# Moving the set-up of the first exponents to VectorE, and a new order, in an mLSTM step followed by a two-layer MLP on one core

## The chip, the cores and the metric

The kernel runs on one core of a Trainium2 chip. The time is device microseconds (us) of that core, the median of three runs. The core's engines work side by side and meet through semaphores: TensorE (PE) multiplies matrices and writes PSUM, VectorE (DVE) and ScalarE (ACT) do elementwise work, GpSimd (POOL) some masks and set-up, and SyncE (SP) issues the DMAs. A release in the profile is an engine, or a DMA, that another one had waited for.

## The reference

First an mLSTM recurrence over 768 steps for 4 batches and 8 heads of 40 numbers, with a running maximum `m` that keeps the exponents in range; its 3072 x 320 output goes through an MLP with 2048 hidden columns.

```python
for t in range(S):
    m_new = np.maximum(f_gate[:, :, t] + m, i_gate[:, :, t])
    f_stab = np.exp(f_gate[:, :, t] + m - m_new)
    i_stab = np.exp(i_gate[:, :, t] - m_new)
    m = m_new
    C = f_stab * C + i_stab * np.einsum('bhd,bhe->bhde', vt, kt)
    n = f_stab * n + i_stab * kt
    y[:, :, t] = sigmoid(o_gate) * (C @ qt) / np.maximum(np.abs(n @ qt), 1.0)
h = x @ w_in                      # x: y as 3072 x 320
g = h * erf(softplus(h))
out = g @ w_out
```

The weights come as 64-bit words. The kernel decodes them to 32 bits on VectorE and ScalarE.

## The kernel before

The 768 steps are cut into 12 chunks (steps) `c` of 64. A step's work for batches 0 and 1, and for 2 and 3, are its halves `r` = 0 and 1. In `attention(c)` the recurrence becomes matrix products: `scores` multiplies q and k into `S`; VectorE multiplies `S` by `dm`, the exponentials of gate differences (L681); `before` adds what the state of earlier steps gives, and the next state's part (L635, L640); `heads` multiplies by v (L649). Then VectorE divides (`den`, L710 to L718), applies the output gate (L724), and copies the last 64 columns of each row once more (L725), so that three 128-wide transposes (`turned`, L510) can bring the result into the layout of the MLP. ScalarE and VectorE split each transposed result into a high and a low part, `xh` and `xl` (L519, L523), since the products run in a format with fewer bits: two or three products replace one.

`mlp(g)` takes 48 groups: four per step, each with a quarter `q` of the hidden columns. A group is two up-projections of 16 matmuls into `h` (L858), two copies `hb` (L866), softplus and erf on ScalarE (L870, L874; each table change costs an ACT_TABLE_LOAD), a multiplication on VectorE (L878), a split into `gh` and `gl`, and the down products into the banks of `pob`, one per 128 tokens: L919 and L920 (`gh`) and L917 (`gl`). The first six groups (`PLAIN`) aren't split and use L915. After a step's last quarter ScalarE copies the bank into `o` (L925), and two DMAs bring it out. Each weight block `raw` is decoded by L740, L746, L751 and L753 and split by L763 and L767 (`w_in`; L801 and L805 for its last 64 rows) or L827 and L831 (`w_out`).

Steps 0 and 1 make their exponents by a matmul of `lt` and `xd` (L562), whose operands `gate_block(0)` builds on VectorE from the gates `gt`, with the selectors `sel`, `one` and `heads_of`. Later steps send theirs through DRAM (`gd`) and read them back as `dm` and `eT`.

The order of all engines' instructions is computed when the kernel is built. `Plan` lists operations with an engine, a cost, what they read and write and a due time, and runs them through a list scheduler: at each moment every free engine takes the ready operation that is due first. `SHIFT`, a table with a number per part and engine, is added to the due times. For TensorE, `fetch` counts instructions: each `BLOCK` of them takes at least `FETCH` us before the next can begin. Where TensorE would be idle for more than `GAP`, `fillers` says how many matmuls on `ident` are put in (`stay`, L983); before the first down product one of them is 128x512. Each engine runs its instructions strictly in the order that results.

At the start GpSimd makes `one` (L355, L357), `ident`, `m0` and `keep` (L347 to L349), zeroes `state` (L384) and then computes `sel` from the constants `cst` (L362 to L370). ScalarE finishes `one` with it (L375), VectorE makes `heads_of` (L379).

Of the kernel before, what the change touches and what calls it, by code (L numbers as in the profile page):

```python
# [10 lines left out]
F32 = mybir.dt.float32  # L11
# [23 lines left out]
class Plan:  # L35
# [5 lines left out]
    GAP, FILL, WIDE_FILL = 0.9, 0.6, 0.85  # L41
    BLOCK, FETCH, SPREAD, SAME = 634, 5.0, 8.0, 1.0
# [84 lines left out]
    def run(self, switch, stay=None):  # L127
# [9 lines left out]
        self.block = 0, -10.0  # L137
# [22 lines left out]
        while count < n:  # L160
# [19 lines left out]
            for e in ('PE', 'DVE', 'ACT', 'POOL', 'SP'):  # L180
# [46 lines left out]
                if e == 'PE':  # L227
                    opened = opened or bool(o.name) and o.name[:2] == 'dn'
                    gap = now - idle
                    if gap > self.GAP and idle > 0:  # L230
                        at, begun = self.block
                        at += 10 * self.fillers(gap, opened)
                        self.block = (at % self.BLOCK, now) if at >= self.BLOCK else (at, begun)
                    if mode is not None and o.kind != mode:
                        cost += 0.2
                    mode = o.kind
                    end, self.block = self.fetch(now, cost, o.mm)
                    cost = end - now
                    idle = end
# [33 lines left out]
WIN = [50, 50, 50, 50, 50, 50]  # L273
WOUT = [50, 50, 50, 50]
LAG = 9.772298661887838
STEPS = [0.39055807994090763, 48.51524298161213, 47.54329309094079, 80.07669209656675, 112.61009110219268, 145.14349010781865, 177.67688911344462, 210.21028811907055, 242.7436871246965, 275.27708613032246, 307.8104851359484, 340.34388414157434]
FIRST, FIRST_X = ((0, 1), (2, 3), (4, 5), (6, 7)), (2, 3)
EACH, LAST = ((0, 1), (2, 3)), ((0, 1), (2,), (3,))
PLAIN, JOIN, GH_ACT = 6, 3, 16


def nominal(g):
    return FIRST_DUE[g] if g < 8 else FIRST_DUE[7] + EVERY * (g - 7)


@with_exitstack
def tile_mlstm_moe(
# [41 lines left out]
    keep = cp.tile([128, W], F32, name="keep")
    one = cp.tile([128, 2, L], F32, name="one")  # L330
    sel = cp.tile([128, 4 + B], F32, name="sel")
    heads_of = cp.tile([128, H], F32, name="heads_of")
    state = [cp.tile([128, 2, NPR, V1], F32, name=f"state{r}") for r in range(2)]
    wh = cp.tile([128, 3, DFF], F32R, name="wh")
    wl = cp.tile([128, 2, DFF], F32R, name="wl")
    woh = cp.tile([128, NFF, DM], F32R, name="woh")

    accs = []
    pob = ps.tile([128, 2, 512], F32, name="pob")

    @dma(6, w=[('cst', 0)], due=-900.0)
    def _():
        nc.sync.dma_start(cst, consts)

    @op('POOL', 0.2, w=[('m0', 0)])
    def _():
        nc.gpsimd.memset(m0, -1e30)  # L347
        nc.gpsimd.memset(keep, 1.0)
        nc.gpsimd.memset(keep[:, L:L + 1], 0.0)  # L349

    @op('POOL', 2.2, w=[('one', 0)], due=-80.0)
    def _():
        for b in reversed(range(B)):
            rows = 32 * (b + 1)
            nc.gpsimd.memset(one[0:rows], 0.0)  # L355
            for i, (test, fill) in enumerate(((ALU.not_equal, 1.0), (ALU.is_ge, -1e30))):
                nc.gpsimd.affine_select(out=one[0:rows, i], in_=one[0:rows, i], pattern=[[1, L]],  # L357
                                        compare_op=test, fill=fill, base=16 * b + 16, channel_multiplier=-1)

    @op('POOL', 1.3, r=[('cst', 0)], w=[('is', 0)], due=-70.0)  # L360
    def _():
        nc.gpsimd.tensor_tensor(sel[:, 1:2], cst[:, 9:10], cst[:, 8:9], op=ALU.subtract)  # L362
        nc.gpsimd.tensor_tensor(sel[:, 0:1], cst[:, 10:11], cst[:, 8:9], op=ALU.add)
        nc.gpsimd.tensor_tensor(sel[:, 2:3], sel[:, 0:1], sel[:, 1:2], op=ALU.add)
        nc.gpsimd.tensor_scalar(out=sel[:, 3:4], in0=sel[:, 2:3], scalar1=-1.0, scalar2=1.0, op0=ALU.mult, op1=ALU.add)
        of = sel[:, 4:4 + B]
# [49 lines left out]
    def gate_block(c):  # L416
# [4 lines left out]
        @dma(128, w=[(('gt', c), 0)], tile_=('gt', ('gt', c)))  # L421
        def _():
            nc.sync.dma_start(new('gt', [128, 2, W], ('gt', c)), gates[:, :, rows])
# [626 lines left out]
```

## Time and profile before

| what | us |
|---|---|
| median of three runs (480.41 to 481.48) | 481.37 |
| the profiled execution, its own time | 479.99 |
| its span | 478.3 |
| TensorE busy, share of the span | 456.3, 95% |
| VectorE busy | 322.0, 67% |
| ScalarE busy | 313.6, 66% |
| GpSimd busy | 48.2, 10% |
| granted TensorE clock, mean | 0.993 |

A share over the whole span hides that stages differ. A later table gives the busy time by stage; there, an engine whose busy time fills the stage sets the pace in it. In a group's row stand the line, the engine, the operation, what is written `<-` what is read, the count, then the busy time, the mean ns of one, and the idle time before it with what ended it. Matmuls overlap one another, so their mean ns is more than what one adds. A float32 matmul is recorded twice, so a filler has two records.

### The profile page before, as it was taken

The numbers are of one execution on the slowest core, as the hardware profiler recorded it, in microseconds if no ns is written. First come the engines' busy times: TensorE is split into PE (matmuls) and PEld (weight loads), VectorE is DVE, ScalarE is ACT, GpSimd is POOL, SyncE is SP. The second block draws the span as 40 slices with busy tenths as digits, with TensorE's granted clock in tenths as the row PEclk, the third lists the DMA queues.
The fourth block names the chain that finished last, engine by engine and source line by source line (L and its number), as shares of the span: only waits on it lengthen the run. The fifth ranks groups of instructions, "written<-read, shape, count | busy, mean of one in ns | idle before, by whom it ended". The sixth has DMA issues, their size and how long they took to land.

```text
span 478.3 us, 14687 instructions
## 1 busy us (share of the span) xinstructions
PE 456.3 (95%) x6482; PEld 421.5 (88%) x6482; DVE 322.0 (67%) x574; ACT 313.6 (66%) x433; POOL 48.2 (10%) x71
## 2 busy tenths in 40 slices
PE   6788999899999999999999999999999999999996
PEld 2457878678999999999899999999999999999985
DVE  4889999999988378367639557769069551554280
ACT  3636799948598399648179288396287272894760
POOL 4000002101203003002101101104003100000000
PEclk9979999999999999999999999999999999999999
DMA  8997835332362433033324313604040300000011
GB/s 282 313 307 224 270 123 170 105 116 78 115 169 66 134 128 129 18 116 107 93 108 128 104 29 108 171 14 143 7 127 21 116 16 1 2 14 15 1 27 29
DMA packets 42476, 50.77 MB, mean 106 GB/s; under 512 B 22700, under 2 KB 27308, under 8 KB 42412
## 3 DMA queue, kind: packets, MB, share of 16 engines
q1 hardware_dynamic: 42412, 49.83, 34.6%
q8 instruction: 51, 0.84, 0.7%
q14 instruction: 13, 0.11, 0.1%
HBM read 45.68 MB, written 4.13 MB: 104 GB/s over the span
## 4 chain that ended last, share of the span: by engine, by line
PE 82%; DVE 8%; ACT 7%; issue 2%; POOL 1%; POOLq 0%; ACTq 0%; DVEq 0%
PE h L858 35%; PE pob L919 10%; PE pob L917 10%; PE pob L920 9%; PE pa L649 3%; PE pob L983 3%; PE pa L635 2%; PE pa L626 2%; PE pob L915 2%; PE pa L915 2%; ACT L985 2%; DVE raw L751 1%; PE pa L510 1%; PE pa L640 1%; ACT n L870 1%
## 5 line engine op out<-in xcount | busy, mean ns | idle before, releaser
L858 PE MATMUL h<-xh,wh 128*128 128x256 f32 x576 | 159.6, 288 | 0.0
L858 PE MATMUL h<-xl,wh 128*128 128x256 f32 x576 | 156.7, 283 | 0.0
L858 PEld LDWEIGHTS h<-xh,wh 128*128 128x128 f32 x576 | 110.0, 191 | 1.9 <-ACT hb L866 0.6
L858 PEld LDWEIGHTS h<-xl,wh 128*128 128x128 f32 x576 | 110.2, 191 | 0.7 <-DVE vg L614 0.2
L866 ACT ACTIVATE hb<-h 128x512 f32<-128x512 f32 x96 | 56.4, 593 | 81.9 <-PE h L858 81.8
L858 PE MATMUL h<-xh,wl 128*128 128x256 f32 x384 | 108.6, 283 | 0.1
L919 PE MATMUL pob<-woh,gh 128*128 128x320 f32 x328 | 99.4, 315 | 1.6 <-ACT o L925 1.6
L920 PE MATMUL pob<-wo,gh 128*128 128x320 f32 x328 | 97.5, 309 | 0.0
L878 DVE TENSOR_TENSOR n<-n,hb 128x1024 f32<-128x1024 f32 x48 | 58.7, 1231 | 40.9 <-ACT n L874 40.8
L985 ACT ACT_TABLE_LOAD x61 | 78.3, 1283 | 1.8 <-PEq L1038 0.8
L604 POOL TENSOR_SCALAR_AFFINE_SELECT dm<-dm 128x512 f32<-128x512 f32 (+1 forms) x40 | 42.5, 1069 | 322.6 <-ACT dm L583 321.3
L858 PEld LDWEIGHTS h<-xh,wl 128*128 128x128 f32 x384 | 73.4, 191 | 0.3 <-DVE wl L767 0.3
L919 PEld LDWEIGHTS pob<-woh,gh 128*128 128x128 f32 x328 | 61.6, 188 | 3.5 <-ACT o L925 2.4
L917 PE MATMUL pob<-woh,gl 128*128 128x320 f32 x328 | 61.0, 314 | 1.8 <-ACT o L925 1.6
L920 PEld LDWEIGHTS pob<-wo,gh 128*128 128x128 f32 x328 | 61.6, 188 | 0.0
L894 DVE TENSOR_TENSOR gl<-n,gh 128x1024 fp32r<-128x1024 f32 x42 | 52.1, 1245 | 2.0 <-ACT gh L888 1.0
L917 PEld LDWEIGHTS pob<-woh,gl 128*128 128x128 f32 x328 | 50.4, 188 | 3.4 <-ACT o L925 2.4
L870 ACT ACTIVATE n<-hb 128x1024 f32<-128x1024 f32 x48 | 50.6, 1058 | 1.2
L874 ACT ACTIVATE n<-n 128x1024 f32<-128x1024 f32 x48 | 49.5, 1053 | 0.2
L710 DVE TENSOR_SCALAR den<-pa 128x8 f32<-128x8 f32 x24 | 3.9, 161 | 46.8 <-PE pa L649 45.8
L925 ACT ACTIVATE o<-pob 128x320 f32<-128x320 f32 x22 | 9.3, 435 | 32.6 <-PE pob L917 26.3
L681 DVE TENSOR_TENSOR dm<-pa,dm 128x512 f32<-128x512 f32 x24 | 16.5, 687 | 20.0 <-PE pa L626 17.3
(94 smaller groups left out, 537.0 us busy)
## 6 DMA issues: line engine op xcount, KB each, us to landing
qk<-in_qk_dram SPq DMA_DIRECT2D x24, 512.0 KB
kvo<-in_kvo_dram SPq DMA_DIRECT2D x24, 484.0 KB
raw<-in_w_out_dram SPq DMA_DIRECT2D x16, 320.0 KB
dm<-gd SPq DMA_DIRECT2D x40, 128.0 KB
raw<-in_w_in_dram SPq DMA_DIRECT2D x8, 512.0 KB
out_dram<-o SPq DMA_DIRECT2D x48, 80.0 KB
eT<-gd SPq DMA_DIRECT2D x22, 128.0 KB
eT<-gd SPq DMA_DIRECT2D x22, 80.0 KB
```

Source lines behind the costliest of these rows:

```text
L604: nc.gpsimd.affine_select(out=x, in_=x, pattern=[[0, H], [1, L]], compare_op=ALU.is_ge, fill=0.0, base=base, channel_multiplier=-1)
L858: nc.tensor.matmul(h[:, n * T:(n + 1) * T], w, m, start=(s == 0), stop=(s == len(ops) - 1))
L866: nc.scalar.activation(G('hb')[:, hs], G(f'h{i}'), AF.Copy)
L870: nc.scalar.activation(new('n0', [128, 1024], ('n0', g)), G('hb'), AF.Softplus)
L874: nc.scalar.activation(G('n0'), G('n0'), AF.Erf)
L878: nc.vector.tensor_tensor(G('n0'), G('n0'), G('hb'), op=ALU.mult)
L894: nc.vector.tensor_tensor(new('gl', [128, 1024], ('gl', g), F32R), G('n0'), G('gh').bitcast(F32), op=ALU.subtract)
L915: nc.tensor.matmul(acc(b), G('n0')[:, ts], t['wo', j], start=(j == 0), stop=(j == NFF - 1))
L917: nc.tensor.matmul(acc(b), G('gl')[:, ts], woh[:, j], start=False, stop=(j == NFF - 1))
L919: nc.tensor.matmul(acc(b), G('gh')[:, ts], woh[:, j], start=(j == 0), stop=False)
L920: nc.tensor.matmul(acc(b), G('gh')[:, ts], t['wol', j], start=False, stop=False)
L985: order = plan.run(lambda k: nc.scalar.preload_act_table_set(KIND[k]), stay)
```

## The change

Seven parts:

1. `sel` and `heads_of` are computed by six operations on VectorE instead of eight on GpSimd and one on VectorE. What of it doesn't hang on `cst` (`own`, two selections) GpSimd prepares. `one` is selected from one zeroed tile, without a memset per block.
2. The gates' DMA for step 0 gets a due time of -950, so it stands right behind that of `cst`.
3. The copy of 64 columns (before L725) goes from VectorE to ScalarE.
4. `WIDE_FILL` falls from 0.85 to 0.65: fewer fillers for a gap of the same length, before the first down product aside.
5. `fetch` counts instruction blocks of 640 (634 before), starts the count at 157.5, takes 4.4 instead of 5.0 us for a block, and lets the loading of a block begin 160 instructions before the end of the last.
6. Costs and due times of the set-up operations are changed.
7. `SHIFT` has new numbers throughout, and so nearly every engine has a new order.

```diff
-    GAP, FILL, WIDE_FILL = 0.9, 0.6, 0.85
-    BLOCK, FETCH, SPREAD, SAME = 634, 5.0, 8.0, 1.0
+    GAP, FILL, WIDE_FILL = 0.9, 0.6, 0.65
+    BLOCK, LEAD, FETCH, SPREAD, SAME = 640, 160, 4.4, 8.0, 1.0
...
-        at, begun = self.block
-        while at + mm >= self.BLOCK:
-            n = self.BLOCK - at
-            now = max(now + cost * n / mm, begun + self.FETCH)
-            cost, mm, at, begun = cost * (mm - n) / mm, mm - n, 0, now
+        at, begun, mark = self.block
+        while True:
+            lim = self.BLOCK - self.LEAD if at < self.BLOCK - self.LEAD else self.BLOCK
+            if at + mm < lim:
+                return now + cost, (at + mm, begun, mark)
+            n = lim - at
+            if mm:
+                now, cost, mm = now + cost * n / mm, cost * (mm - n) / mm, mm - n
+            at = lim
+            if lim < self.BLOCK:
+                mark = now
+            else:
+                late = begun + self.FETCH > now
+                now = max(now, begun + self.FETCH)
+                begun, at = now if late else mark, 0
             if not mm:
-                break
-        return now + cost, (at + mm, begun)
+                return now + cost, (at, begun, mark)
...
-        self.block = 0, -10.0
+        self.block = 157.5, -10.0, -10.0
...
-SHIFT = {'g0:SP.9': -36.6, 'g0:DVE.10': 56.3,
...
+SHIFT = {'g0:SP.9': 897.9, 'g0:DVE.10': 42.8,
...
-    @op('POOL', 0.2, w=[('m0', 0)])
+    @op('POOL', 0.45, w=[('m0', 0)], due=-90.0)
...
-    @op('POOL', 2.2, w=[('one', 0)], due=-80.0)
+    @op('POOL', 0.8, w=[('own', 0)], due=-85.0)
     def _():
+        nc.gpsimd.memset(own, 1.0)
+        nc.gpsimd.affine_select(out=own, in_=own, pattern=[[-32, B]], compare_op=ALU.is_ge, fill=0.0, base=0, channel_multiplier=1)
+        nc.gpsimd.affine_select(out=own, in_=own, pattern=[[32, B]], compare_op=ALU.is_ge, fill=0.0, base=31, channel_multiplier=-1)
+
+    @op('POOL', 2.3, w=[('one', 0)], due=-80.0)
+    def _():
+        nc.gpsimd.memset(zero, 0.0)
         for b in reversed(range(B)):
             rows = 32 * (b + 1)
-            nc.gpsimd.memset(one[0:rows], 0.0)
             for i, (test, fill) in enumerate(((ALU.not_equal, 1.0), (ALU.is_ge, -1e30))):
-                nc.gpsimd.affine_select(out=one[0:rows, i], in_=one[0:rows, i], pattern=[[1, L]],
+                nc.gpsimd.affine_select(out=one[0:rows, i], in_=zero[0:rows], pattern=[[1, L]],
...
-    @op('POOL', 1.3, r=[('cst', 0)], w=[('is', 0)], due=-70.0)
+    @op('DVE', 0.7, r=[('cst', 0), ('own', 0)], w=[('is', 0), ('hd', 0)], due=-70.0)
     def _():
-        nc.gpsimd.tensor_tensor(sel[:, 1:2], cst[:, 9:10], cst[:, 8:9], op=ALU.subtract)
...
+        nc.vector.tensor_tensor(sel[:, 1:2], cst[:, 9:10], cst[:, 8:9], op=ALU.subtract)
+        nc.vector.tensor_tensor(sel[:, 0:1], cst[:, 10:11], cst[:, 8:9], op=ALU.add)
+        nc.vector.tensor_tensor(sel[:, 2:3], sel[:, 0:1], sel[:, 1:2], op=ALU.add)
+        nc.vector.tensor_scalar(out=sel[:, 3:4], in0=sel[:, 2:3], scalar1=-1.0, scalar2=1.0, op0=ALU.mult, op1=ALU.add)
+        nc.vector.tensor_scalar(out=sel[:, 4:4 + B], in0=own, scalar1=sel[:, 2:3], scalar2=sel[:, 3:4], op0=ALU.mult, op1=ALU.add)
+        nc.vector.tensor_scalar(out=heads_of, in0=cst[:, 0:H], scalar1=sel[:, 2:3], scalar2=sel[:, 3:4], op0=ALU.mult, op1=ALU.add)
...
-        @dma(128, w=[(('gt', c), 0)], tile_=('gt', ('gt', c)))
+        @dma(128, due=(-950.0 if c == 0 else None), w=[(('gt', c), 0)], tile_=('gt', ('gt', c)))
...
-                nc.vector.tensor_copy(A('kvo', r)[:, KV + 320:KV + 384], A('kvo', r)[:, KV + 256:KV + 320])
+                if not ACT_TWICE:
+                    nc.vector.tensor_copy(A('kvo', r)[:, KV + 320:KV + 384], A('kvo', r)[:, KV + 256:KV + 320])
+
+            if ACT_TWICE:
+                @op('ACT', 0.24, w=[K('kvo', r, 'o')])
+                def _(r=r):
+                    nc.scalar.activation(A('kvo', r)[:, KV + 320:KV + 384], A('kvo', r)[:, KV + 256:KV + 320], AF.Copy)
```

What the new order does is seen in the engines' instructions, in the order in which they run. The first place is VectorE at the start, up to the operands of the first exponents; before, from its first operation on:

```order
L379 TENSOR_SCALAR heads_of<-cst,sel 128x8
L431 COPY m<-m_66 128x1
L432 SCALAR_TENSOR_TENSOR m<-gt,m_66 128x128
L441 TENSOR_TENSOR x<-gt,m 128x128
L442 TENSOR_TENSOR x<-x,m 128x128
L444 MEMSET x 128x1
L445 SCALAR_TENSOR_TENSOR x<-keep,x 128x128
L446 TENSOR_TENSOR x<-gt,m 128x128
L448 TENSOR_TENSOR x<-x 128x128
L450 SCALAR_TENSOR_TENSOR x<-x,sel,one 128x128 x2
L471 TENSOR_TENSOR xd<-x,heads_of 128x512
L464 TENSOR_TENSOR lt<-x,sel 128x256 x2
```

Of the changed kernel, behind the six operations of part 1, the copy of `m` and its scan (the line numbers are its own, 17 or more higher):

```order
L763 TENSOR_SCALAR raw<-raw 128x320
L458 TENSOR_TENSOR x<-gt,m 128x128
L459 TENSOR_TENSOR x<-x,m 128x128
L461 MEMSET x 128x1
L462 SCALAR_TENSOR_TENSOR x<-keep,x 128x128
L463 TENSOR_TENSOR x<-gt,m 128x128
L465 TENSOR_TENSOR x<-x 128x128
L467 SCALAR_TENSOR_TENSOR x<-x,sel,one 128x128 x2
L481 TENSOR_TENSOR lt<-x,sel 128x256 x2
L774 SCALAR_TENSOR_TENSOR raw<-raw 128x320
L776 SCALAR_TENSOR_TENSOR wo<-raw 128x320
L488 TENSOR_TENSOR xd<-x,heads_of 128x512 x2
```

A whole decode of a `w_out` block (L763, L774, L776) has moved in, and `lt` stands ahead of `xd`. In the rest of the first stretch the decodes of three more `w_out` blocks and one split stand ahead of the second `xl` of step 0, where one decode stood before. On SP that block's DMA comes right behind those of `cst` and the gates; before, the order was `cst`, the first `qk`, the gates.

The second place is TensorE from its first instruction to step 0's exponents; before:

```order
L392 MATMUL pob<-ident 128x512
L983 MATMUL pob<-ident 128x512 x6
L562 MATMUL pa<-xd,lt 128x512 x2
L626 MATMUL pa<-qk 64x64 x32
L562 MATMUL pa<-xd,lt 128x512
```

And changed:

```order
L409 MATMUL pob<-ident 128x512
L1006 MATMUL pob<-ident 128x512 x4
L579 MATMUL pa<-xd,lt 128x512 x3
L643 MATMUL pa<-qk 64x64 x32
L579 MATMUL pa<-xd,lt 128x512
```

Two fillers less, and the third product of `lt` and `xd` has moved ahead of the scores. Behind this place the fillers stand in runs of 3, 2, 1 and 2 before, and of 1, 3, 1, 1, 2 and 4 in the changed kernel; the first up-projection comes behind all of `S`, `turned` and the first `heads` of step 1 instead of ahead of those `heads`, and the run of 4 stands between eight up-projections and the first down products.

The third place is TensorE near the end, where the down products pass from step 10 to step 11, with the semaphores that an instruction waits for; before:

```order
L920 MATMUL pob<-wo,gh 128x320
L917 MATMUL pob<-woh,gl 128x320 [waits DVE_49]
L917 MATMUL pob<-woh,gl 128x320 x7
L919 MATMUL pob<-woh,gh 128x320 [waits Activation_49]
L920 MATMUL pob<-wo,gh 128x320
```

And changed:

```order
L881 MATMUL h<-xh,wl 128x256
L881 MATMUL h<-xh,wh 128x256
L881 MATMUL h<-xl,wh 128x256
L942 MATMUL pob<-woh,gh 128x320 [waits DVE_49,Activation_49]
L943 MATMUL pob<-wo,gh 128x320
```

The wait for ScalarE's copy of a bank came right behind products into the other bank; now an up-projection of 16 matmuls stands between, and the wait behind its last.

More of the change, by code (lines that the diff above doesn't have):

```diff
@@ L230, in run @@
                     if gap > self.GAP and idle > 0:
-                        at, begun = self.block
-                        at += 10 * self.fillers(gap, opened)
-                        self.block = (at % self.BLOCK, now) if at >= self.BLOCK else (at, begun)
+                        at, begun, mark = self.block
+                        for _ in range(self.fillers(gap, opened)):
+                            was, at = at, at + 10
+                            if was < self.BLOCK - self.LEAD <= at:
+                                mark = now
+                            if at >= self.BLOCK:
+                                at, begun = at - self.BLOCK, mark
+                        self.block = at, begun, mark
                     if mode is not None and o.kind != mode:
@@ L279 @@
 PLAIN, JOIN, GH_ACT = 6, 3, 16
+ACT_TWICE = True
 def nominal(g):
@@ L332, in tile_mlstm_moe @@
     heads_of = cp.tile([128, H], F32, name="heads_of")
+    own = cp.tile([128, B], F32, name="own")
+    zero = cp.tile([128, L], F32, name="zero")
     state = [cp.tile([128, 2, NPR, V1], F32, name=f"state{r}") for r in range(2)]
@@ L361, in _ @@
     def _():
[L362 to L366, printed above, removed]
-        nc.gpsimd.tensor_copy(of, sel[:, 2:3].to_broadcast([128, B]))
-        nc.gpsimd.affine_select(out=of, in_=of, pattern=[[-32, B]], compare_op=ALU.is_ge, fill=0.0, base=0, channel_multiplier=1)
@@ L369, in _ @@
-        nc.gpsimd.affine_select(out=of, in_=of, pattern=[[32, B]], compare_op=ALU.is_ge, fill=0.0, base=31, channel_multiplier=-1)
-        nc.gpsimd.tensor_scalar(out=of, in0=of, scalar1=sel[:, 3:4], scalar2=None, op0=ALU.add)
-    @op('ACT', 0.5, r=[('is', 0)], w=[('one', 0)], due=-60.0)
+        nc.vector.tensor_tensor(sel[:, 1:2], cst[:, 9:10], cst[:, 8:9], op=ALU.subtract)
+        nc.vector.tensor_tensor(sel[:, 0:1], cst[:, 10:11], cst[:, 8:9], op=ALU.add)
+        nc.vector.tensor_tensor(sel[:, 2:3], sel[:, 0:1], sel[:, 1:2], op=ALU.add)
@@ L373, in _ @@
+        nc.vector.tensor_scalar(out=sel[:, 3:4], in0=sel[:, 2:3], scalar1=-1.0, scalar2=1.0, op0=ALU.mult, op1=ALU.add)
+        nc.vector.tensor_scalar(out=sel[:, 4:4 + B], in0=own, scalar1=sel[:, 2:3], scalar2=sel[:, 3:4], op0=ALU.mult, op1=ALU.add)
+        nc.vector.tensor_scalar(out=heads_of, in0=cst[:, 0:H], scalar1=sel[:, 2:3], scalar2=sel[:, 3:4], op0=ALU.mult, op1=ALU.add)
+    @op('ACT', 0.8, r=[('is', 0)], w=[('one', 0)], due=-60.0)
     def _():
@@ L375, in _ @@
             nc.scalar.activation(one[:, i], one[:, i], AF.Identity, scale=sel[:, 3:4], bias=sel[:, i:i + 1])
-    @op('DVE', 0.1, r=[('is', 0), ('cst', 0)], w=[('hd', 0)], due=-60.0)
-    def _():
-        nc.vector.tensor_scalar(out=heads_of, in0=cst[:, 0:H], scalar1=sel[:, 2:3], scalar2=sel[:, 3:4], op0=ALU.mult, op1=ALU.add)
     @op('POOL', 0.8, w=[('st', r) for r in range(2)])
@@ L719, in _ @@
                                         A('den', r).unsqueeze(3).to_broadcast([128, 2, NPR, D]), op=ALU.mult)
-            @op('DVE', 0.55, r=[K('kvo', r, 'k')], w=[K('kvo', r, 'o')])
+            @op('DVE', 0.36 if ACT_TWICE else 0.55, r=[K('kvo', r, 'k')], w=[K('kvo', r, 'o')])
             def _(r=r):
```

2 lines of the change are left out of this document (1 added, 1 removed).

## The prediction

> **What bounds the kernel now.** I read the table of stages first: in each stretch of the execution the busy time (and count) of TensorE, its weight loads, VectorE, ScalarE and GpSimd, then the granted clock and the DMA's share and rate.
>
> ```profile
> 0.00:12.20 12.20, 7.92 (x15) 3.47 (x16) 5.61 (x17) 3.87 (x7) 5.71 (x31) 1.00 0.82 279
> 12.20:34.00 21.80, 17.40 (x346) 9.74 (x344) 17.57 (x39) 11.53 (x23) 0.00 (x0) 0.84 1.06 306
> 34.00:49.00 15.00, 12.43 (x319) 10.83 (x318) 14.07 (x36) 8.33 (x16) 0.00 (x0) 1.00 0.84 244
> 49.00:65.00 16.00, 16.00 (x121) 14.69 (x120) 15.17 (x29) 14.00 (x21) 0.00 (x0) 1.00 0.72 236
> 65.00:92.00 27.00, 25.10 (x441) 21.56 (x443) 25.57 (x53) 26.59 (x43) 2.84 (x4) 1.00 0.46 144
> 92.00:127.00 35.00, 33.60 (x296) 27.57 (x284) 33.44 (x67) 23.20 (x38) 6.93 (x8) 1.00 0.29 93
> 127.00:216.00 89.00, 88.47 (x1526) 85.58 (x1529) 58.86 (x106) 64.28 (x84) 8.27 (x8) 1.00 0.36 108
> 216.00:425.00 209.00, 207.75 (x3120) 201.76 (x3120) 130.22 (x211) 133.05 (x172) 24.48 (x20) 1.00 0.25 74
> 425.00:474.30 49.30, 47.66 (x342) 46.32 (x340) 21.48 (x23) 28.32 (x36) 0.00 (x0) 1.00 0.08 18
> ```
>
> There are two regimes. From 127 us on TensorE is the bound: 88.47 of 89.0, 207.75 of 209.0, 47.66 of 49.3 us, while VectorE has a third free. It idles 3.4 us there in all. Between 12.2 and 127 us VectorE is the bound: 105.8 of 114.8 us, the five rows added up; it decodes the weights while attention's first steps need it too. TensorE's busy time there is flattered by fillers, matmuls on `ident` whose result nobody reads. The list of groups (busy time, mean ns) has them:
>
> ```profile
> L983 PE MATMUL pob<-ident 128*128 128x512 f32 x28 | 16.0, 714 | 0.0
> ```
>
> Of these 16.0 us 6.2 lie before 12.3 (timeline below), so 9.8 lie behind. With 10.3 us of idle time in the five rows, TensorE gives away about 20 us between 12.2 and 127, and 12.2 before that. Whatever is gained ahead of 127 us is carried to the end, since behind it TensorE alone sets the pace. The list of who waited for whom tells which waits these are:
>
> ```profile
> PE pa L510 <- DVE kvo L718: 2.1, 1, 2.1
> PE pob L917 <- ACT o L925: 1.6, 3, 0.5
> PE pob L919 <- ACT o L925: 1.6, 3, 0.5
> PE pob L915 <- issue: 0.8, 1, 0.8
> ```
>
> (Total, times, longest.) The six waits for L925 make up 3.2 of the 3.4 us that TensorE loses behind 127: it waits until ScalarE has copied one bank of `pob` out, though it goes on in the other.
>
> **The start.** The timeline (start, duration, engine, what):
>
> ```profile
> 0.79 0.39 SPq L343 DMA_DIRECT2D cst<-in_consts_dram  x1
> 1.71 0.69 SPq L423 DMA_DIRECT2D gt<-in_gates_dram  x1
> 4.28 2.08 PE L392 MATMUL pob<-ident 128*128 128x512 f32 x2 [4.28 <-POOL ident masks.py:199]
> 4.50 0.68 POOL L384 MEMSET state<- 128x328 f32 x2
> 5.14 0.19 POOL L362 TENSOR_TENSOR sel<-cst 128x1 f32<-128x1 f32 x1
> 6.07 0.29 DVE L379 TENSOR_SCALAR heads_of<-cst,sel 128x8 f32<-128x8 f32 x1 [6.07 <-POOL sel L365]
> 6.14 6.20 PE L983 MATMUL pob<-ident 128*128 128x512 f32 x12
> 6.33 0.48 DVE L432 TENSOR_TENSOR_SCAN m<-gt,m 128x128 f32<-128x128 f32 x1
> 7.26 0.67 ACT L746 ACTIVATE raw<-raw 128x512 f32<-128x512 f32 x1 [0.41 <-DMA raw<-in_w_in_dram]
> 9.46 0.69 DVE L471 TENSOR_TENSOR xd<-x,heads_of 128x512 f32<-128x512 f32 x1
> 10.07 0.75 DVE L464 TENSOR_TENSOR lt<-x,sel 128x256 f32<-128x256 f32 x2
> 12.18 1.88 PE L562 MATMUL pa<-xd,lt 128*128 128x512 f32 x4
> ```
>
> Now VectorE's first work waits until 6.07 for `sel` from GpSimd, and GpSimd begins `sel` at 5.14 because two memsets stand ahead of it, not because `cst` is late. No row shows when `cst` lands: not before its issue ends at 1.2, not after 5.14. The nearest row is the first `raw`: 1158 KB are issued up to it (6, 512, 128 and 512 by the code), it lands at 7.26, and at the 279 GB/s of the first stage these bytes take 4.15 us; so a few KB at the head of the queue land near 3.1, my value. The gates, now 128 KB behind them, land by 3.6.
>
> The change has VectorE begin at 3.1 instead of 6.07, with five small operations more. The small operations of `den` are the nearest rows:
>
> ```profile
> L710 DVE TENSOR_SCALAR den<-pa 128x8 f32<-128x8 f32 x24 | 3.9, 161 | 46.8 <-PE pa L649 45.8 <-ACT state L704 1.0
> L740 DVE TENSOR_SCALAR raw<-raw 128x320 int32<-128x320 int32 x16 | 5.3, 352 | 0.0
> L751 DVE SCALAR_TENSOR_TENSOR raw<-raw 128x320 int32<-128x320 int32 x16 | 8.3, 518 | 0.4
> L753 DVE SCALAR_TENSOR_TENSOR wo<-raw 128x320 int32<-128x320 int32 x16 | 7.9, 493 | 0.6
> L831 DVE TENSOR_TENSOR wo<-wo,woh 128x320 fp32r<-128x320 f32 x16 | 9.4, 585 | 0.1
> L725 DVE COPY kvo<-kvo 128x64 f32<-128x64 f32 x24 | 5.7, 238 | 0.8
> ```
>
> Five at 0.2 with the step between them are 1.0, so the scan of `m` starts about 1.9 earlier than 6.33. Into the chain to the first operands now come one `w_out` decode (0.35 + 0.52 + 0.49 = 1.36) and both `lt` (0.75) ahead of `xd`: its first half ends at 10.15 - 1.9 + 1.36 + 0.75 = 10.4. TensorE has two fillers less, four records of 6.20 / 12 = 0.52, and starts them about 0.3 later (my estimate for five small operations that GpSimd now has ahead of `ident`, less the memsets of `one`): 12.18 - 2.1 + 0.3 = 10.4. Before, the fillers ended 1.4 us behind the operands (12.18 against 10.82); now they meet near 10.5. **Term 1: -1.9**, since VectorE, the bound, is ahead by that and TensorE's fillers no longer hide it. The bounds: +0.2 (`cst` at 5.14, `xd` at 12.4) and -3.8 (`cst` at 1.2).
>
> **The copies given to ScalarE.** 24 x 0.238 = 5.7 us leave VectorE, but only the six of steps 0 to 2 while it is the bound: 1.4. ScalarE, which takes them at about the same price, is itself 26.59 of 27.0 busy between 65 and 92, and `turned` now waits for it. **Term 2: -1.0**; bounds -1.4 and, where the copy queues behind a ScalarE instruction that waits, +1.0.
>
> **The new order up to 127 us.** Here VectorE's own waits are at stake, and where the first products stand:
>
> ```profile
> DVE n L878 <- ACT n L874: 1.3, 2, 0.7
> DVE vg L614 <- ACT dm L567: 1.2, 1, 1.2
> DVE xl L523 <- ACT xh L519: 1.2, 1, 1.2
> DVE den L710 <- ACT state L704: 1.0, 2, 0.6
> L597 DVE TENSOR_TENSOR qe<-qk,eT 104x512 f32<-104x512 f32 x22 | 16.3, 746 | 2.9 <-DMA eT<-gd 2.7 <-DMA gd<-x 0.2
> 33.39 0.56 DVE L523 TENSOR_TENSOR xl<-pa,xh 128x384 fp32r<-128x384 f32 x1 [1.16 <-ACT xh L519]
> 33.99 0.68 PE L858 MATMUL h<-xh,wh 128*128 128x256 f32 x1
> ```
>
> These four waits (up to 130 us) sum to 4.7. The second `xl` at 33.39 lets the first up-projection go at 33.99. Ahead of that `xl` VectorE now has three `w_out` decodes more (4.1), one split (0.59), one `qe` (0.75) and the set-up (1.0), less two copies (0.5): 5.9 of work, brought forward. With the 2.9 of the start that puts it at 36.4, if the waits until then (1.2 + 1.2 + 1.0) stay, and at 33.0 if the work brought forward fills them all. In return step 1's first heads, which followed the first 32 products, now stand ahead of the first up-projection, and the decodes are out of the way later. So nothing is lost by a first product at 35; what counts is how many of the 4.7 us are filled. **Term 3: -1.5**, a third of them, because TensorE still meets the same producers; bounds -4.7 and +3.0 (36.4 against 33.4, never made good).
>
> **The hand-over of the banks.** A row of the chain of work that ended last prices what can hide such a wait (start, duration, sixteen up-projection matmuls):
>
> ```profile
> 114.42 1.91 PE h L858 x16
> ```
>
> Behind 127 us the new order has five such waits. Two stand behind 16 up-projection matmuls, one behind a step's `heads`, one behind three transposes, and one, the last, right behind the products of the other bank. The six waits are 0.53 each (3.2 / 6), so 1.91 hides one whole. **Term 4: five of six, -2.6**; bounds 0 (ScalarE, with 24 instructions more, is late with the copy) and -3.2.
>
> **Fillers and instruction blocks.** Behind the first operands there are 12 fillers instead of 8, four of them in a row ahead of the first plain down product, where two stood. Four more are eight records of 0.52, 4.1 us. In a wait they cost nothing, and the 10.3 us of idle time are more than twice that, so I take a quarter. **Term 5: +1.0**, bounds 0 and +4.1. That the planner now places instruction blocks otherwise can save what the waits call "issue", the 0.8 shown; I take 0. [...]
>
> **The sum.** -1.9 - 1.0 - 1.5 - 2.6 + 1.0 = -6.0. The profiled execution took 479.99 us (span 478.3 and 1.7 around it), so 474.0; the runs' median of 481.37 is 1.4 above it: 475.4.
>
> **Rivals.** (a) *Slower: the first products come late.* If `cst` lands only at about 5.1, VectorE gains nothing at the start, carries 5.9 us of early decodes, and reaches the second `xl` at 36.4 or later; TensorE meets its up-projections 3.0 late and runs the added fillers (4.1) besides: 0.2 + 3.0 + 4.1 - 1.0 - 2.6 = +3.7, 485.1. It decides at a second `xl` behind about 36. For it: VectorE is saturated there. Against it: GpSimd's own queue explains 5.14.
> (b) *Only local gains*: the lead is used up by TensorE's waits for the same producers: -1.0 - 2.6 + 1.0 = -2.6, 478.8.
> (c) *The change does not do what it says*: `cst` sets the start as before, and each wait removed comes back under another name, the bank copies behind a fuller ScalarE: 0, 481.4.
> (d) *The clock falls.* The stage from 12.2 to 34 had a granted clock of 0.84: between waits TensorE goes to half rate there. Fewer fillers early and single ones between waits might extend this to the first 25 up-projection matmuls, 0.12 each by the row of sixteen, so 3.0 more at half rate: -6.0 + 3.0, 478.4. [...]
>
> **How the numbers follow.** Forecast 0.58, (b) 0.14, (d) 0.07, (c) 0.09, (a) 0.12. A measurement of this kernel can tell about 0.2% from no change, 480.4 to 482.3. Faster: 0.58 + 0.14 + 0.07 = 0.79; same 0.09; slower 0.12. The forecast's own range is 469.5 (terms 3 and 1 near their best ends) to 479; to leave out no more than 2 in 10 it goes up over (b), (c) and (d) to 482.5, which leaves (a) and the far low ends outside.
>
> **What would show it.** VectorE's first operation on `sel` near 3.1, first product on `xd` near 10.5 (not 12.2); the second `xl` at 33 to 36; less than 4 us of these waits of VectorE up to 130; one or two waits for the bank copy behind 127 us instead of six; TensorE's matmuls beginning to run without gaps some 4 us earlier, and everything behind at the same pace. The prediction is wrong if `sel` starts near 5, if TensorE idles longer between 50 and 75 than the fillers cover, or if new waits of ScalarE appear behind the added copies.

## The result, and the profile after

| what | before | changed |
|---|---|---|
| median of 15 runs each, us | 481.54 (480.08 to 483.51) | 485.49 (482.88 to 487.63) |
| ratio, 95% interval | 1 | 1.0075 (1.0053 to 1.0097) |
| the profiled execution, its span | 479.99, 478.3 | 482.91, 481.2 |

The changed kernel is 0.75% slower, some 3.6 us by the ratio (the medians are 3.95 apart), and not 6 us faster: 485.49 against a forecast of 475.4 with a range up to 482.5. Its profiled execution is one of its shortest, 2.6 below its median, so its profile shows the loss rather too small. Three executions of the experiments below, one of e1 and two of e9 with the profiled one among them, were over 1.5% longer than the shortest of their kernel; they are left out of the ratios.

The table of stages of the changed kernel, in the stretches of the first one (us, busy time and count of TensorE, its weight loads, VectorE, ScalarE and GpSimd, granted clock, the DMA's share and GB/s):

```profile
0.00:12.20 12.20, 8.16 (x13) 3.61 (x14) 8.28 (x26) 5.19 (x10) 3.68 (x23) 1.00 0.77 275
12.20:34.00 21.80, 16.33 (x340) 8.81 (x339) 16.11 (x37) 11.54 (x24) 0.00 (x0) 0.84 1.07 331
34.00:49.00 15.00, 10.09 (x285) 7.64 (x284) 11.44 (x26) 5.47 (x11) 0.00 (x0) 0.93 0.93 259
49.00:65.00 16.00, 16.00 (x123) 15.34 (x122) 12.88 (x30) 12.28 (x22) 0.00 (x0) 0.95 0.52 136
65.00:92.00 27.00, 27.00 (x309) 22.59 (x309) 24.28 (x47) 25.76 (x41) 3.11 (x4) 1.00 0.44 143
92.00:127.00 35.00, 34.24 (x340) 28.09 (x339) 30.99 (x63) 25.33 (x40) 3.16 (x4) 1.00 0.31 93
127.00:216.00 89.00, 87.99 (x1511) 84.80 (x1510) 61.87 (x108) 68.17 (x96) 11.36 (x12) 1.00 0.36 104
216.00:425.00 209.00, 208.10 (x3199) 201.45 (x3198) 127.27 (x201) 127.61 (x176) 20.23 (x20) 1.00 0.28 81
425.00:474.30 49.30, 49.30 (x369) 49.12 (x367) 24.26 (x24) 35.78 (x40) 0.00 (x0) 1.00 0.05 11
```

What was VectorE's stage is so no longer: between 12.2 and 49 it works 27.6 us instead of 31.6, TensorE 26.4 instead of 29.8, ScalarE 17.0 instead of 19.9. They stand still together. From 127 on TensorE is as full as it was. The list of who waited for whom says for what (total, times, longest):

```profile
PE pa L666 <- issue: 7.5, 3, 3.7
PE pob L942 <- ACT o L948: 1.0, 3, 0.5
PE pob L940 <- issue: 0.8, 1, 0.8
PE pa L652 <- DVE xl L540: 1.0, 1, 1.0
```

The waits for the bank copies have gone as expected, 3.2 to 1.0. In their stead stands "issue", time in which the engine waits for nothing that the profile shows: 8.3 us in four waits, where it was 1.2 in two. The timeline shows where (start, duration, engine, what, idle time before):

```profile
2.48 0.25 DVE L386 TENSOR_TENSOR sel<-cst 128x1 f32<-128x1 f32 x1 [2.48 <-DMA cst<-in_consts_dram]
...
11.13 2.83 PE L579 MATMUL pa<-xd,lt 128*128 128x512 f32 x6
...
21.18 0.30 PE L666 MATMUL pa<-kvo,dm 64*32 64x41 f32 x9
25.03 1.18 PE L666 MATMUL pa<-kvo,dm 64*32 64x41 f32 x55 [3.55 <-issue]
...
26.80 0.17 DVE L727 TENSOR_SCALAR den<-pa 128x8 f32<-128x8 f32 x1 [3.34 <-ACT state L721]
...
37.43 0.55 DVE L540 TENSOR_TENSOR xl<-pa,xh 128x384 fp32r<-128x384 f32 x1
...
43.09 0.56 PE L666 MATMUL pa<-kvo,dm 64*32 64x41 f32 x35
47.38 0.76 PE L666 MATMUL pa<-kvo,dm 64*32 64x41 f32 x29 [3.74 <-issue]
...
48.66 0.41 PE L881 MATMUL h<-xh,wl 128*128 128x256 f32 x1
48.88 0.41 PE L881 MATMUL h<-xh,wh 128*128 128x256 f32 x1
...
50.53 0.28 PE L881 MATMUL h<-xh,wh 128*128 128x256 f32 x1
50.65 0.28 PE L881 MATMUL h<-xl,wh 128*128 128x256 f32 x1
```

The set-up did what it was to do: VectorE begins at 2.48, and the first product of `xd` comes at 11.13 instead of 12.18. Then TensorE stops in the middle of `heads`, behind the ninth of 64 equal matmuls, for 3.55 us, and again behind the 35th for 3.74. Nothing differs between one of these matmuls and the next. The wait doesn't stay with TensorE: ScalarE's `state` and, behind it, VectorE's `den` need these `heads`, and so VectorE, the bound of this stage in the kernel before, stands still for 3.34 us ahead of 26.80.

What runs out are the instructions. The list of DMA queues has a queue for them (packets, MB, share of 16 engines):

```profile
q1 hardware_dynamic: 42412, 49.83, 34.9%
q8 instruction: 51, 0.84, 0.7%
```

51 packets of 16 KB, for 12,972 recorded matmuls and weight loads of TensorE (6486 of each): a piece of some 256 instructions a packet. Counted from the first instruction, semaphores included, the first wait stands ahead of number 449 and the second ahead of 1217, three times 256 later. In the kernel before, its two waits "issue" stood ahead of 449 and 2497. All are 193 and a multiple of 256. So are all 26 waits of this name of 0.7 us or more in the traces of both kernels and the twelve experiments. These waits stand where one piece of 256 ends and the next begins, and the one at 47.38 lasted 3.74 us.

Read from the trace's records of these packets, with the KB that SP had issued and that had not yet moved when TensorE entered the piece before (times in us):

```
kernel   piece  piece before   KB     packet starts   packet   next in-    wait
         begins entered        queued  after entry     ends     struction
before     449     17.56         843      2.13          20.69     21.93     0.43
before    1217     39.56         437      1.63          42.12     44.05     none
changed    449     18.11        1975      4.40          23.62     25.03     3.55
changed    705     25.03        1565      3.60          29.74     33.36     none
changed   1217     39.67        2268      5.24          45.95     47.38     3.74
```

In these rows the packet of a piece starts 1.6 to 5.2 us after the piece before it is entered, the later the more data is queued then (437 to 2,268 KB); in the three with a wait TensorE goes on 1.2 to 1.4 us after the packet has landed. Elsewhere the fetch begins a little earlier: of 700 packets in the traces of both kernels and the twelve experiments (the first 50 of each) 268 started ahead of the entry, none by more than 42 instructions. In attention TensorE runs through 256 small instructions in 3.2 us (18.11 to 21.28), while the fetch takes 4.4 + 1.1 + 1.4. The piece entered at 25.03 holds fillers: the packet of the next one landed at 29.74, and its first instruction came at 33.36 without a wait.

To set the runs side by side I gave each matmul of TensorE what it adds when nothing waits (an up-projection matmul 0.12 us, a filler 0; 422.6 in all) and read when the same share of work was done:

```
work done, us      6      40      60      150     350     422.4
before           20.65   71.59   96.97  190.28  398.45   473.78
changed          -0.06   +7.30   +2.96   +4.93   +3.67    +2.90
e1 (below)       -0.46   +4.30   -0.05   +1.84   +0.86    +0.07
e3               -1.38   -1.67   -1.13   -1.16   -1.26    -1.26
e6               -0.29   +4.59   +0.25   +4.71   +4.65    +3.88
e7               -1.48   -1.72   -2.68   -1.94   -4.45    -6.92
```

The changed kernel loses 7.3 us up to 40, gets 4.3 back up to 60 and keeps 2.9. That the 4.3 come from the decodes being out of the way is my reading; no run shows it.

### The profile page after: what moved, and what is told of

Read it like the earlier page. It is cut to its first block, busy times and chain, and to the rows that moved or that the text cites. A ratio compares the mean times of both kernels' runs of the same rounds, so it can differ in the third digit from the quotient of the medians.

```text
span 481.2 us, 14681 instructions
## 1 busy us (share of the span) xinstructions
PE 459.5 (95%) x6486; PEld 423.2 (88%) x6486; DVE 317.4 (66%) x555; ACT 318.0 (66%) x457; POOL 41.5 (9%) x63
## 4 chain that ended last, share of the span: by engine, by line
PE 83%; DVE 8%; issue 3%; ACT 3%; DMA 1%; POOL 0%; SPq 0%; DVEq 0%; POOLq 0%
PE h L881 36%; PE pob L942 10%; PE pob L940 10%; PE pob L943 9%; PE pa L666 3%; PE pob L1006 3%; PE pa L652 3%; PE pa L643 2%; PE pa L938 2%; PE pa L657 2%; PE pa L527 1%; DVE raw L774 1%; PE pob L938 1%; DMA raw<-in_w_out_dram 1%; DVE wo L776 1%
## 5 line engine op out<-in xcount | busy, mean ns | idle before, releaser
L621 POOL TENSOR_SCALAR_AFFINE_SELECT dm<-dm 128x512 f32<-128x512 f32 (+1 forms) x40 | 37.9, 952 | 328.9 <-ACT dm L600 252.6
L666 PE MATMUL pa<-kvo,dm 64*32 64x41 f32 x1536 | 20.9, 202 | 7.5 <-issue 7.5
L666 PEld LDWEIGHTS pa<-kvo,dm 64*32 64x32 f32 x1536 | 17.6, 109 | 11.1 <-issue 9.8
```

Of the source, the lines that this page charges most:

```text
L621: nc.gpsimd.affine_select(out=x, in_=x, pattern=[[0, H], [1, L]], compare_op=ALU.is_ge, fill=0.0, base=base, channel_multiplier=-1)
L666: nc.tensor.matmul(y[os, j, p], w[ds, j, p, ts], v[ds, 2 * p + j], start=False, stop=(p == NPR - 1))
```

## The experiments

Two theories stand against one another. F: TensorE waits for its instructions, which come behind the queued data, and the new order has put dense runs of small matmuls where the queue is long. N: the order itself, or something in the dense runs, costs the time, wherever the pieces begin and whatever SP does. Medians, and ratios to the kernel before with their 95% intervals, are of 6 to 12 runs. The kernel before ran beside each, with medians of 481.26 to 482.42, so experiments are best set against one another by their ratios.

**e3: the set-up alone.** The kernel before, with parts 1 and 2 of the change.

```diff
-        nc.gpsimd.tensor_tensor(sel[:, 1:2], cst[:, 9:10], cst[:, 8:9], op=ALU.subtract)
...
+        nc.vector.tensor_tensor(sel[:, 1:2], cst[:, 9:10], cst[:, 8:9], op=ALU.subtract)
...
+        order[n], order[n - 1] = order[n - 1], order[n]
...
+        order[first] = (0, lambda: stay(4), None)
```

The first of the two lines on `order` puts the gates' load ahead of that of `qk`, the second takes 4 fillers instead of 6.

> The kernel before with parts 1 and 2 of the change alone, in the old order, and four fillers instead of six ahead of the first product. Term 1 of the prediction: first product at 10.3-11.2 instead of 12.18, VectorE ahead by 2, median 1.9 lower (479.6). F adds: the piece boundary falls 8 instructions later in the work and more may be queued when the piece is entered earlier, so the 0.43 us wait in the first heads grows to 1-2.5 and eats the lead: 480.5-482.

478.93, 0.9946 (0.9929 to 0.9963): 2.6 us faster. Its timeline:

```profile
10.77 1.88 PE L563 MATMUL pa<-xd,lt 128*128 128x512 f32 x4
...
19.85 0.33 PE L650 MATMUL pa<-kvo,dm 64*32 64x41 f32 x11
21.16 0.72 PE L650 MATMUL pa<-kvo,dm 64*32 64x41 f32 x53 [0.98 <-issue]
```

The first product comes 1.4 earlier than before and the wait for instructions grows to 0.98, nearly as F had it; but F had also said that this would eat the lead (480.5 to 482), and the lead reaches the end (-1.3 in the profile). So parts 1 and 2 gain, and the rest of the change loses 485.49 - 478.93 = 6.6.

**e1: the transfers held back.** In the changed kernel, a 4-byte transfer makes SP wait at two places.

```diff
+            (0, lambda: nc.sync.dma_start(zero[0:1, 0:1], wh.bitcast(F32)[0:1, 1, 0:1]), None)] + late + order[s + 1:]
...
+        order.insert(p, (0, lambda: nc.sync.dma_start(zero[0:1, 1:2], t['dm', 1, 1][0:1, 0, 0:1]), None))
```

The first stands ahead of `w_in`, `kvo`, `w_out`, `gd` and `qk` of step 1 and waits for the second `wh`; the other stands ahead of `qk` of step 3 and all behind it and waits for `dm` of step 1.

> The changed kernel, same order on every engine, but SP holds its bulk transfers back twice, by a 4-byte transfer that reads a tile written about 18 us (the second wh) and about 39.5 us (dm of step 1), so that less is queued when TensorE enters the two pieces of 256 instructions after which it stood still 3.55 and 3.74 us. Theory F (a piece's instructions are fetched behind the bytes already issued): about 650 and 480 KB instead of 1,900 and 2,280 are ahead, so the waits fall below 1.2 and below 0.5 us and the median falls from 485.5 to 478.5-480.5. Theory N (the dense run of small matmuls itself costs the time, whatever SP does): both waits stay at about 3.6, and the time stays at 485-486.

482.58, 1.0013 (0.9990 to 1.0036): 2.9 below the changed kernel. With 267 KB queued at 17.70 the packet started after 0.84 us, and the 64 matmuls run through; with 1,446 KB queued at 38.26 the second wait is 2.0:

```profile
20.78 0.86 PE L666 MATMUL pa<-kvo,dm 64*32 64x41 f32 x64
21.57 2.84 PE L1006 MATMUL pob<-ident 128*128 128x512 f32 x6
...
22.98 0.16 DVE L727 TENSOR_SCALAR den<-pa 128x8 f32<-128x8 f32 x1
...
27.55 1.14 PE L643 MATMUL pa<-qk 40*64 40x64 f32 x32 [3.14 <-DVE wo L854]
...
44.23 0.64 PE L666 MATMUL pa<-kvo,dm 64*32 64x41 f32 x29 [2.00 <-issue]
```

That speaks against N, though the time isn't the 478.5 to 480.5 that F named, and the second wait isn't under 0.5. With the first wait gone VectorE reaches the second `den` at 22.98 instead of 26.80. The new wait of 3.14 at 27.55 is the price of the hold, though the row names VectorE's L854: by the trace's semaphores TensorE waits there for the first `qk` of step 1, which was issued at 20.85 instead of 17.53 and landed at 27.41. In e6 (below), where nothing is held back, that load lands at 25.20 and the same scores begin at 25.41.

**e5: held back more finely.** As e1, but one `w_in` block that isn't needed before 50 us goes later, and less is held back.

```diff
+        later(('i30:SP', 193), ('i10:SP', 129))
+        later(('i30:ACT', 195), ('m1:ACT', 231))
...
+        order.insert(p, (0, lambda: nc.sync.dma_start(zero[0:1, 1:2], t['den', 1, 0][0:1, 0, 0:1]), None))
```

The block's step on ScalarE moves with it. Of step 1 only one `w_out` block and the three `qk` now wait for `wh`; `qk` of step 3 waits for `den` of step 1.

> The changed kernel with the transfers held back more finely than in e1: one w_in block that nothing needs before 50 us goes later on SP, and the two 4-byte transfers hold back only one w_out block and the three qk at 18 us, and qk and all behind it at 40.8 us, so that some 600 KB stay queued and the queue doesn't run empty. F: both waits for instructions under 1 us and no new wait of 3 us in its place; 5-7 below the changed kernel, 478.5-480.5. N: the time that e1 won came by chance, and this stays at 482-485.

483.19, 1.0020 (0.9995 to 1.0046): a miss for F, and within the time that N named. The first wait is 0.81 (555 KB, packet after 1.71), but TensorE stands 3.59 for VectorE at 36.33, and then 4.89 for the piece that begins at 961: entered at 28.98 with some 1,030 KB queued, its packet started 12.6 us later. The queue at entry doesn't explain that one.

**e6: pieces that begin elsewhere.** The changed kernel, with twelve matmuls of one element where TensorE waits for `ident`; no transfer is touched.

```diff
+            for _ in range(12):
+                nc.tensor.matmul(pob[0:1, 1, 0:1], zero[:, 0:1], zero[:, 0:1], start=True, stop=True)
```

> The changed kernel with twelve matmuls of one element (48 recorded instructions) ahead of TensorE's first filler, where it waits for ident anyway: all pieces of 256 instructions begin 48 instructions earlier in the work, nothing else changes. F, with the queue of the profiled run at the times at which pieces would then be entered, plus 2.4 us: the first wait (3.55) goes to 0-1, the second moves one piece ahead, to some 39.5 us, and is 2.5-3 instead of 3.74: 4-5.5 us less, 480-481.5. N: the place of the boundaries doesn't matter, 485-486.

485.63, 1.0081 (1.0054 to 1.0108): no gain, and the time that N named. The timeline:

```profile
20.94 0.81 PE L666 MATMUL pa<-kvo,dm 64*32 64x41 f32 x64
...
40.16 0.34 PE L666 MATMUL pa<-kvo,dm 64*32 64x41 f32 x11
44.29 0.80 PE L666 MATMUL pa<-kvo,dm 64*32 64x41 f32 x53 [3.79 <-issue]
```

The first wait is gone, the second `xl` of step 0 comes at 34.50 instead of 37.43, and up to 150 us of the execution (100 of work) e6 is 2.7 ahead of the changed kernel. Then pieces that begin 48 earlier fall into `heads` of later steps, with new waits of 1.83 at 149.6 and 1.32 at 198.4, which my sum had left out. By the time alone N would stand; but all its waits for instructions stand where the shifted pieces begin. F is right on where the waits stand and was wrong on their sum.

**e8: the same to the kernel before.** Twenty such matmuls, 80 instructions, and a small memset on GpSimd for what they read.

```diff
+            for _ in range(20):
+                nc.tensor.matmul(pob[0:1, 1, 0:1], zero[:, 0:1], zero[:, 0:1], start=True, stop=True)
```

> The kernel before with twenty matmuls of one element (80 recorded instructions) ahead of TensorE's first filler. F, by the same sum of queue and 2.4 us at the new places of the boundaries: instead of one wait of 0.43 us at 21.9 one of about 4.5 in the first heads or scores near 22.5, so 3-4.5 us slower: 485-486. N: 481-482.

485.16, 1.0076 (1.0051 to 1.0102): 3.8 us slower, and as slow as the changed kernel, in the old order and with the old transfers.

```profile
22.98 0.69 PE L628 MATMUL pa<-qk 40*64 40x64 f32 x31
26.47 0.27 PE L628 MATMUL pa<-qk 40*64 40x64 f32 x1 [2.80 <-issue]
...
93.67 0.49 PE L651 MATMUL pa<-kvo,dm 64*32 64x41 f32 x27
97.01 0.57 PE L651 MATMUL pa<-kvo,dm 64*32 64x41 f32 x37 [2.85 <-issue]
```

The wait of 0.43 has become one of 2.80 ahead of the last of 32 matmuls, and two more of 1.48 and 2.85 stand at 89.9 and 97.0. N has no reason for these places. Two things limit this run. In its profile 1.0 us is lost before attention begins: the first product comes at 13.18 instead of 12.18, since 12 records of fillers took 7.16 us instead of 6.20. e2, whose TensorE instructions up to there are those of the kernel before, shows 12.95, so the start differs between executions of the same code; how much of the median it makes isn't shown. And the 2.85 at 97.0 is no wait behind queued data: the piece before was entered at 89.93 with nothing queued, no data moved from 90.0 to 93.0, and the packet started at 94.44.

**e2: bytes added to the queue.** The kernel before, with an idle transfer of 1,536 KB.

```diff
+        order.insert(at('g4:SP', 477) + 1, (0, lambda: nc.sync.dma_start(spare, w_in.bitcast(I32)[0:96, 0:4096]), None))
```

> The kernel before with one idle transfer more of 1,536 KB (w_in to a spare place in DRAM, read by nobody), issued at about 38.6 us, just before TensorE enters a piece at 39.56. F: 434 + 1,536 KB are ahead of the next piece, 5.2 us at the 390 GB/s of that stretch, and 2.4 us for the piece itself, so TensorE, which needs it at 44.05, stands still until about 47, a new wait of some 3 us in the heads of step 1, and the median goes from 481.5 to 484-486. N: no wait over 0.5 us there and 481-482.5.

484.11, 1.0054 (1.0031 to 1.0076). The new wait is there, at 46.02, but of 0.52 and not 3: the packet started 3.0 after entry, not 5.2. (The 390 GB/s behind the 5.2 is what the kernel before moves from 18 to 24: 402, 370 and 401 in steps of 2 us. From 40 to 44 it moves 205 and 180.) The time is in F's range, but part of the loss was there before the idle transfer was issued, a first product 0.8 later and a first wait of 1.52 with 1,299 KB queued. It supports F in direction only.

**e12: loads earlier.** e7 (below) with three loads moved ahead of the second gates' load.

```diff
+        g = order.pop(at('g2:SP', 337))
+        order.insert(at('i01:SP', 95) + 1, g)
```

> e7 with three loads (qk and kvo of step 1, and a w_in block) moved ahead of the second gates' load on SP, for which SP waits until 14.1: no byte is added, and these loads land earlier. F: some 1,800 instead of 867 KB are queued when TensorE enters the piece at 16.0, so the 1.11 us wait for instructions at 21 grows to 2.3-3.5 and the median goes from 473.6 to 474.5-476. N: earlier loads help or do nothing: 472.5-473.8, the wait at about 1.

473.59, 0.9827 (0.9796 to 0.9858), as e7, and a miss for F. The first of these loads didn't start before 14.17: SP had waited for an earlier load to land, not for the gates. So the queue was 1,295 KB and not 1,800. With it the packet started 2.88 us after entry, as in e7 (2.86) with two thirds of that queued, and no wait for instructions is left. The queue at entry alone doesn't say how late a packet comes.

**e4: the copies back on VectorE**, in the changed kernel.

```diff
-                if not ACT_TWICE:
+                if True:
...
-                    nc.scalar.activation(A('kvo', r)[:, KV + 320:KV + 384], A('kvo', r)[:, KV + 256:KV + 320], AF.Copy)
+                    pass
```

> The changed kernel with the 24 copies of 64 columns back on VectorE, order otherwise the same. Term 2 of the prediction: 1.0 us slower than the changed kernel (486.5). F: VectorE has slack while TensorE waits for instructions, so no more than 0.5 either way (485-486), with the two waits of 3.5 us still there.

489.62, 1.0168 (1.0139 to 1.0197), 4.1 above the changed kernel. Its profile shows waits of 3.00 and

```profile
39.46 0.72 PE L666 MATMUL pa<-kvo,dm 64*32 64x41 f32 x52
47.26 0.48 PE L666 MATMUL pa<-kvo,dm 64*32 64x41 f32 x12 [7.09 <-issue]
```

for the piece that begins at 961, its packet 11.3 us after entry. That is 3.35 more than the second wait of the changed kernel, and no price of a copy.

**e10: the copies alone on ScalarE**, in e7.

```diff
-                nc.vector.tensor_copy(A('kvo', r)[:, KV + 320:KV + 384], A('kvo', r)[:, KV + 256:KV + 320])
+                nc.scalar.activation(A('kvo', r)[:, KV + 320:KV + 384], A('kvo', r)[:, KV + 256:KV + 320], AF.Copy)
```

> e7 with the 24 copies of 64 columns on ScalarE, right behind the gate's multiplication, order otherwise the same: part 3 of the change by itself, where TensorE hardly waits for instructions. Term 2 of the prediction: 1.0 below e7, 472.6. The other way: ScalarE takes a copy only behind its own queue, and turned waits longer: 474.5-477.

473.92, 0.9836 (0.9802 to 0.9871), against 473.64: neither of the two, and no gain where the wait for instructions is small, 1.0 against 1.1 in e7.

**e7: the set-up, and the banks apart.** e3, with `pob` as two tiles.

```diff
-    pob = ps.tile([128, 2, 512], F32, name="pob")
+    pob = [ps.tile([128, 512], F32, name=f"pob{b}") for b in range(2)]
...
-            return t['po', k][:, 512 * b:512 * b + DM] if k == 1 else pob[:, b, 0:DM]
+            return t['po', k][:, 512 * b:512 * b + DM] if k == 1 else pob[b][:, 0:DM]
```

> e3 (old order, set-up on VectorE, gates first) with pob as two tiles, one for each bank, so that a product into one bank no longer waits for ScalarE's copy of the other. If the six waits of 0.53 are what they seem, they go and 3.2 us with them: 475.5-476.5. If they hide another wait behind them (ScalarE's copy needed soon after anyway): 478-479.

473.64, 0.9834 (0.9801 to 0.9867): 5.3 below e3, and the best of all kernels here. The waits of TensorE in e3 had

```profile
PE pob L920 <- ACT o L926: 1.6, 3, 0.5
PE pob L918 <- ACT o L926: 1.6, 3, 0.5
PE pa L511 <- DVE kvo L719: 1.5, 1, 1.5
PE pa L511 <- DVE xl L524: 1.4, 1, 1.4
```

and the list of e7 begins with

```profile
PE pob L393 <- POOL m L349: 3.7, 1, 3.7
PE pa L511 <- DVE kvo L719: 1.6, 1, 1.6
PE pa L636 <- ACT aT L490: 1.6, 1, 1.6
PE pa L627 <- DVE dm L682: 1.4, 2, 0.8
PE pa L641 <- ACT dm L568: 1.3, 2, 0.7
PE pa L650 <- issue: 1.1, 1, 1.1
```

The six waits are gone. In the comparison by equal work each is worth 0.8: from 350 to 422.4, where three of them stood, e7 gains 2.5. So the idle 0.53 isn't all that such a wait cost here; where the other 0.3 come from no run shows.

**e11: the banks apart in the changed kernel**, with the edit of e7.

> The changed kernel with pob as two tiles. Term 4 of the prediction says that the new order has taken nearly all of these waits away (1.0 us of them is left in its profile), so this gains no more than 1.5: 484-485.5. If the new order only moved them: as much as e7 gained over e3, 5 us: 480-481.

484.52, 1.0063 (1.0039 to 1.0087), 1.0 below the changed kernel, with intervals that overlap. It is not the 5 us of e7: the new order had indeed hidden most of these waits. Its second wait for instructions, too, stands at piece 961 and is 5.31, with the same order on TensorE as the changed kernel's 3.74 at 1217:

```profile
38.94 0.72 PE L666 MATMUL pa<-kvo,dm 64*32 64x41 f32 x52
44.97 0.49 PE L666 MATMUL pa<-kvo,dm 64*32 64x41 f32 x12 [5.31 <-issue]
```

So this wait differs between kernels with one order, and, as e9 shows, between executions.

**e9: both remedies.** e6 with the second hold of e5 (qk of step 3 and all behind it wait for den of step 1).

> e6 (the changed kernel, pieces of 256 instructions beginning 48 earlier) and the second hold of e5 (qk of step 3 and what is behind it on SP wait for den of step 1, some 38 us), so that a few hundred KB instead of 1,924 are queued when TensorE enters the piece ahead of the 3.79 us wait. F: that wait under 1 us, the two late waits of e6 (1.83 and 1.32) still there: 482-483, 3 below e6. N: the time comes back at another place, 485-486.

482.09, 0.9991 (0.9960 to 1.0023), 3.5 below e6, as forecast. But its profiled execution, the longest of its runs (477.5 to 485.1), has waits of 3.12 and 4.25 again, with 852 and 1,236 KB queued. It can't stand for the others, so that the hold took the second wait away isn't shown. Up to 38 us e9 does what e6 does, and the profiled execution of e6 had no first wait: the same instructions meet it in one execution and not in another.

## Why the prediction was wrong

**The step that failed** is the one on instruction blocks: "can save what the waits call 'issue', the 0.8 shown; I take 0", with no end above nothing. The row that I quoted for it was the price of a block that came nearly in time; the piece that begins at 449 cost 0.43 before and 3.55 in the changed kernel, its packet 2.13 and 4.40 after entry: the change had moved both the order and the start of the fetch. In the profiled executions the waits went from 1.2 to 8.3, and the first of 3.55 passed on to VectorE, which stood 3.34 for it. Beside the waits stands what followed the second: the granted clock was 0.50 from 47.04, just before it ended, to 50.45 (up-projection matmuls follow each other every 0.21 instead of 0.12, as the rows from 48.66 and from 50.53 show). My row of the stages even showed the DMA's share at 1.06 between 12.2 and 34, and I didn't ask who else needed it. The sum of -6.0 plus the 7.1 of added waits is +1.1, against +2.9 in the profile. The clock's 3.4 us at half rate make at most 1.7 of the rest; how it divides between the clock and the other terms no run shows.

**Term 1** (-1.9): right in kind, e3 gives -2.6. `cst` landed by 2.48, earlier than the 3.1 that I took. The first product of the changed kernel came at 11.13 and not near 10.5; in e1, with the same instructions up to there, it came at 10.24.

**Term 2** (-1.0): no gain, e10 against e7 +0.3 within the intervals. In that kernel the copies' 5.7 us of VectorE brought nothing that these runs can tell.

**Term 3** (-1.5): not reached. The second `xl` came at 37.43, behind the 36 that I had named as the mark of rival (a). But 3.34 of it was VectorE's wait for the late `heads`: in e6, where the pieces begin elsewhere and no transfer differs, the second `xl` comes at 34.50, within the 33 to 36 of the forecast. So the start of the new order was read about right, and the first wait for instructions took it away. What the order would be worth without any wait for instructions wasn't reached by any run.

**Term 4** (-2.6): the waits went nearly as read from the order, 3.2 to 1.0, in three waits and not in one or two. From 150 us of work to the end, where all six stood, the changed kernel gains 2.0 on the one before (+4.93 to +2.90), and e11 finds about 1.0 left. Two tiles, which take the wait away altogether, gained more: 0.8 for each.

**Term 5**: fillers were not tried by themselves.

**Rivals.** (a) had the sign, and its 485.1 is 0.4 from the median, but by luck: `cst` wasn't late, and what held the second `xl` was the wait for instructions. The first up-projection came at 39.93 against 33.99, half of that by the order itself (37.00 in e6). (d) was half right: the clock fell, to 0.50 from 47.04 to 50.45, and 11 up-projection matmuls began in these 3.4 us, not 25. That fewer fillers bring this about no run shows. The 0.84 from 12.2 to 34 isn't a half rate between waits: in both kernels it is one stretch of 6.83 us at 0.50, before from 24.98, within a wait of 2.11, to 31.80, changed from 23.15, within the wait of 3.55, to 29.97; in the first TensorE was busy for 6.16 us of it.

## What to carry to other kernels

Count TensorE's instructions in pieces of 256 and see which pieces run in less time than a fetch takes, 4.4 us here with 843 KB queued and 6.9 with 1,975: there twenty small matmuls more cost 3.8 us (e8), and an "issue" row is the trace of it. A load that was issued long before it was needed wasn't free here: holding such loads back (e1) made the changed kernel 2.9 us faster. What moved the pieces moved the waits too: in e6 the 3.55 went and 1.83 and 1.32 came at other places, in e8 0.43 became 2.80. So the place of one wait is not worth tuning by itself. Before reordering around a wait, see whether its cause is only the grain of a tile: two tiles in place of one gained 5.3 us here, more than the new order was forecast to gain from these waits.

## What I had not expected of the hardware

A fetch of 16 KB started 0.8 us after entry with 267 KB queued, 2.1 with 843, 3.2 with 1,299 and 4.4 with 1,975 (first pieces of e1, the kernel before, e2 and the changed kernel), some 2.1 us more for each MB more. Over the first 50 fetches of all fourteen traces the median delay was 0.8 us with 0.1 to 0.5 MB queued at entry, 2.2 with 0.5 to 1, 3.2 with 1 to 1.5 and 4.0 with 1.5 to 2. But 13 fetches came more than 2.5 us later than a line of 0.5 us plus 2.2 for each MB, near these medians. The longest were 12.6 us with some 1,030 KB (e5), 11.3 with 1,632 (e4) and 8.7 with 1,223 (e11), and seven of the 13 had 30 KB or less queued, as the piece of e8 that came 4.5 us after entry while no data moved for three of them. So the amount queued is one cause of a late fetch (in e1 the same instructions met 267 KB instead of 1,975, and 0.84 us instead of 4.40) and not the only one; the other is open. In every wait for instructions the engine went on 1.2 to 1.6 us after its packet had landed.
